# Loads of the step loop on ACT's queue, and the first FFN weights converted and halved earlier

## The chip, the core and the metric

The program runs on one core of one Trainium2 chip. The metric is the device time of one execution in microseconds, taken as the median of several executions. Before the change it is 673.82 us (three runs, 672.1 to 676.8). TensorE (PE) multiplies matrices into the PSUM banks; VectorE (DVE) and ScalarE (ACT) read and write PSUM and SBUF; GpSimd (POOL) works on SBUF here; the DMA engines move data between memory and SBUF. A transfer is issued by an instruction on the queue of one engine: SP's queue, which does nothing else, or those of ACT and POOL, where the instruction stands in line with that engine's computing.

## What is computed

Attention with mixing across heads ("talking heads"), and behind it two feed-forward stages. For 2 batches, 12 heads, 448 positions and head size 64:

```python
scores = scale * np.matmul(q, k.transpose(0, 1, 3, 2))
scores = np.einsum('bhij,hg->bgij', scores, w_pre)        # mix heads before the softmax
attn = np.exp(scores - np.max(scores, axis=-1, keepdims=True))
attn = attn / (np.sum(attn, axis=-1, keepdims=True) + 1e-09)
attn = np.einsum('bhij,hg->bgij', attn, w_post)           # mix heads behind it
x = np.matmul(attn, v)                                    # then laid out as 896 x 768
g = x @ w_gate                                            # 768 x 1536
y = (g * sigmoid(g) * (x @ w_val)) @ w_out                # 1536 x 768
h = y @ w_in                                              # 768 x 2048
out = (h * np.clip(h + 3.0, 0.0, 6.0) / 6.0) @ w_out2     # 2048 x 768
```

The feed-forward (FFN) weights come in as 64-bit numbers and are turned into 32-bit ones on the chip.

## The kernel before

**The loop of steps.** The 2 x 448 query positions are cut into 8 tiles `t` (4 for each batch) and these into 90 chunks of 10 positions; a step takes two chunks, so the loop `for i in range(-LOOK, NP)` has steps 0 to 44 behind a prologue. Three tiles of work are in flight, each at another stage. For its own pair of chunks step `i` does `postmix` (56 matmuls into `ppost`, weights `wn` times exponentials `e`) and copies the result out (`attn_out`, into `at`, half on DVE and half on ACT). For the next pair it has `exps(i+1)` on ACT (tile `e`, with its sums) and `weights(i+1)` on DVE (`rc`, `wn`). For the pair after that it has `premix(i+2)` on PE (`ppre`, from the relaid scores `sx`) and `row_max(i+2)` on DVE (`nm`, which `exps` needs). Beside these a step may hold one head pair of a later tile's scores (`qk`: PE into `pqk`, then one copy each on DVE and ACT into `S`) and one of an earlier tile's product with the values (`av` and `av_rest` on PE into `pav`; `xs` or, in the last two tiles, `xh` on ACT and `xl` on DVE). The second part of `av_rest` waits for a small DVE instruction (`turns`, L348). No step from 36 on has scores. In this document **step i begins with the first matmul of its `postmix`** (L287).

**The order of each engine** is the order in which the code is written (the schedule is manual). What a step does outside its fixed part hangs in the lists `extra[i][place]`; `run(i, place)` writes them out, and `"end"` stands last in a step, behind `out` (`xs`) and before the next step's `exps`.

**Transfers.** `relayout` moves a chunk's scores from `S` into `sx` on SP's queue (104 rows, 182 KB), `relayout_rest` the rest on POOL's (42 KB). Up to six pairs are held in `sx`. The tiles `S0` and `S1` are each used for every second `t`, so the first copy of a new tile's scores waits for all relayouts out of the old one. Loads of queries, keys, values and FFN weights are called from the list `loads` as (step, function, arguments) and go to SP's queue too, between relayouts. In the built program the transfers of SP and ACT share eight semaphore lanes (DMAHW0 to 7) in turn; each waits until the one before it on its lane has landed.

**The first FFN weights.** `fetch`, `convert` and `halve` bring in, convert and split the weights: `convert` is an `Abs` on ACT and four DVE passes (L490), `halve` makes the rounded part on ACT (L427, `hg`, `hv`) and the remainder (`lg`, `lv`; for the first two on POOL). For the first two of the 64 pieces (`j` = 0 and 1: `rg`, `rv`), each cut in thirds, this is spread over steps; one raw tile in the pool `early` serves both. The space of `halve`'s result (`wp0`) is opened at step 41, when the pool of `S` is closed. From then on single FFN matmuls of the first products (`p`, L441) can be put between the attention's: `fill(n)` writes n of them, `FILL` says how many at the last three steps, and two calls `fill(10)` stand in the tail behind the loop. There are 72 in the two products; what is not filled in runs after the tail.

**After the loop** comes a tail with the rest of `av`, and then the FFN: pieces `g`/`v` (12 each), `o` (12), `i` (16) and `p` (18).

Of the kernel before, what the change touches and what calls it, by code (L numbers as in the profile page):

```python
# [9 lines left out]
I64 = mybir.dt.int64  # L10
# [34 lines left out]
FILL = (0, 6, 0)  # L45
# [3 lines left out]
def kernel(  # L49
# [39 lines left out]

    small = kp.tile([128, 8], F32, name="small")  # L90
# [12 lines left out]
    def load_q(t, c0=0, c1=HP, eng=nc.sync):  # L103
        b, i = divmod(t, 4)
        n = ROWS[b][i]
        if c0 == 0:
            qs[t] = pq.tile([128, HP * STRIDE * KI], F32, name=f"q{t}", tag="q")
        base = HP * sum(ROWS[b][:i])
        eng.dma_start(out=qs[t][:, c0 * n : c1 * n], in_=qT[b, :, base + c0 * n : base + c1 * n])

    def load_k(b, c0, c1, eng=nc.sync):
        eng.dma_start(out=ks[b][:, c0:c1, :], in_=kT[b, :, c0 * S : c1 * S].rearrange("p (c j) -> p c j", j=S))
# [4 lines left out]
    def load_v(b, j):  # L117
        nc.sync.dma_start(
            out=vs[b][:, j].rearrange("p h d -> p (h d)"), in_=vv[b, :, j * DM : (j + 1) * DM]
        )  # L120

    new_k(0)
    load_q(0, 0, 2)
    load_k(0, 0, 1, nc.scalar)
    load_k(0, 1, 2)
    load_q(0, 2, 4, nc.scalar)
    load_k(0, 2, 3)
    load_k(0, 3, 4, nc.scalar)
    load_k(0, 4, 5)
    load_q(0, 4, 6, nc.scalar)  # L130
    load_k(0, 5, 6)
    load_q(1)
# [4 lines left out]
    load_q(2)  # L137
    new_v(0)
    for j in range(2):
        load_v(0, j)  # L140
# [258 lines left out]
    def load_w(pool, src, kc, name):  # L399
        st = pool.tile([128, kc, 128], I64, name=f"r{name}", tag="wr", bufs=1 if pool is pools["early"] else 2)  # L400
        n = 2 if pool is pools["early"] else kc
        return st, [(st[:, k : k + n, :], src[:, k : k + n, :]) for k in range(0, kc, n)]
# [70 lines left out]
    def fetch(j, which="wp"):  # L473
        if j < len(subs):
            kind, idx, k0, kc, src = subs[j]
            if j not in raws:
                raws[j] = pools[which], *load_w(pools[which], src, kc, f"{kind}{idx}_{k0}")
            to, of = raws[j][2].pop(0)
            nc.sync.dma_start(out=to, in_=of)

    def convert(j, part=None):
        if j < len(subs):
            kind, idx, k0, kc, _ = subs[j]
            if j not in ys:
                pool, st, _ = raws[j]
                ys[j] = pool, *convert_w(pool, st, kc, f"{kind}{idx}_{k0}")
            todo = ys[j][2]
            for _ in range(len(todo) if part is None else part):
                f, *args = todo.pop(0)
                f(*args)  # L490
# [75 lines left out]
    FREE = {(5, 2): "pqk", (5, 4): "pqk", (6, 0): "pqk", (6, 2): "pqk"}  # L566
# [27 lines left out]
    loads = [(1, load_v, 0, 2), (2, load_v, 0, 3), (3, load_q, 3), (6, load_q, 4)]  # L594
    loads += [(7 + n, load_k, 1, n, n + 1) for n in range(HP)]
    loads += [(15, load_q, 5), (21, load_q, 6), (27, load_q, 7)]
    loads += [(20 + 2 * j, load_v, 1, j) for j in range(JC)]
    loads += [(n, fetch, 0, "early") for n in (14, 17, 19)] + [(n, fetch, 1, "early") for n in (30, 32, 34)]
# [3 lines left out]
    for j in range(2):  # L602
        for n in range(12):
            at_step(17 + 14 * j + n, convert, j, 2 if n % 4 == 0 else 1)
# [10 lines left out]
    for i in range(-LOOK, NP):  # L615
# [25 lines left out]
        if i >= NP - 3:  # L641
            fill(FILL[i - NP + 3])
        run(i, "qk")
        run(i, "out2")
        if i == 41:
            late.close()
            pools["wp0"] = ctx.enter_context(tc.tile_pool(name="wp0", bufs=2, side="right"))
        if i in (42, 43):
            halve(i - 42)
# [9 lines left out]
        while rests < placed and rests // 2 <= i + LOOK + 4 and i > scored[chunks[rests][0]]:  # L659
            relayout_rest(rests)  # L660
            rests += 1
    last = [(6, 4), (6, 5)] + [(7, c) for c in range(HP)]
# [176 lines left out]
```

## Time and profile before

| | before |
|---|---|
| median of three runs | 673.82 us (672.1 to 676.8) |
| the profiled execution: its own time | 673.18 us |
| its span, first to last instruction | 671.4 us |
| PE busy | 660.2 us, 98% |
| DVE, ACT, POOL busy | 499.4, 296.0, 160.3 us |
| granted TensorE clock, mean | 1.000 |

The rest of this text speaks of microseconds from the start of the span. The prologue lasts to 20.56, the loop to 170.49 plus its last step, the tail to 182.80, and the FFN to the end. A matmul's end is modelled, so a "busy" PE may be PE that waits with its last matmul; waits are read from the idle time behind an instruction, `[idle before <-releaser]`, and from the chain of work that ended last.

### The profile page before, as it was taken

How to read it: one execution, taken by the hardware profiler on the slowest of the kernel's cores; microseconds unless marked ns; L12 is line 12 of the kernel's file. 1: busy time of each engine (PE TensorE's matmuls, PEld its weight loads, DVE VectorE, ACT ScalarE, POOL GpSimd, SP SyncE). 2: the span in 40 equal slices, each digit the busy share in tenths (PEclk: the TensorE clock that was granted, in tenths of full speed). 3: DMA queues.
4: the chain of work that ended last, by engine and by line, in shares of the span. 5: the costliest groups of instructions: out<-in, count | busy, mean ns of one | idle time of the engine just before them, and what ended most of it. 6: DMA issues, size and time to landing. Idle time of an engine off the chain costs nothing.

```text
span 671.4 us, 16136 instructions
## 1 busy us (share of the span) xinstructions
PE 660.2 (98%) x6680; PEld 563.2 (84%) x6680; DVE 499.4 (74%) x835; ACT 296.0 (44%) x603; POOL 160.3 (24%) x204
## 2 busy tenths in 40 slices
PE   8989999999999999999999999999999999999997
PEld 3456666666899999999999999999999998999997
DVE  4878889889288888888787666578888888765550
ACT  4667667777234343343432323244444553332220
POOL 3544365445211113111120000013333332000000
PEclk9999999999999999999999999999999999999999
DMA  7767566645023333242333333323222333553420
GB/s 247 213 202 207 189 194 199 184 139 206 12 94 110 127 112 124 95 140 95 108 128 95 108 127 107 128 73 115 95 96 95 108 112 92 167 169 119 152 67 27
DMA packets 35081, 86.87 MB, mean 129 GB/s; under 512 B 10080, under 2 KB 22896, under 8 KB 35008
## 3 DMA queue, kind: packets, MB, share of 16 engines
q1 hardware_dynamic: 26496, 81.21, 37.5%
q0 software_dynamic: 7936, 3.94, 2.4%
q8 instruction: 52, 0.85, 0.5%
q10 hardware_dynamic: 576, 0.70, 0.3%
q14 instruction: 21, 0.17, 0.1%
HBM read 62.37 MB, written 2.75 MB: 97 GB/s over the span
## 4 chain that ended last, share of the span: by engine, by line
PE 76%; DVE 17%; ACT 3%; DMA 3%; issue 1%; SPq 0%; ACTq 0%
PE pp L441 15%; PE po L441 13%; PE pv L441 12%; PE pg L441 12%; DVE yi L490 9%; PE ppost L287 5%; PE ppre L239 5%; PE pqk L171 5%; PE pav L318 5%; DVE rl L727 2%; PE p L441 2%; PE pav L337 2%; DVE yp L490 2%; DVE li L432 2%; ACT hi L427 2%; DMA v<-in_v_dram 1%
## 5 line engine op out<-in xcount | busy, mean ns | idle before, releaser
L441 PE MATMUL pp<-g,hp 128*128 128x448 f32 x384 | 107.8, 362 | 0.0
L703 POOL TENSOR_TENSOR g<-rl,g 128x448 fp32r<-128x448 f32 x32 | 41.3, 1314 | 167.8 <-ACT g L702 167.8
L441 PE MATMUL po<-u,ho 128*128 128x448 f32 x288 | 81.4, 363 | 0.0
L441 PEld LDWEIGHTS pp<-g,hp 128*128 128x128 f32 x384 | 71.9, 187 | 5.4 <-ACT hp L427 0.2
L261 ACT ACTIVATE e<-ppre,nm 128x448 f32<-128x448 f32 x90 | 56.3, 630 | 34.6 <-DVE nm L252 34.5
L441 PE MATMUL pp<-g,lp 128*128 128x448 f32 x192 | 69.7, 363 | 0.2 <-DVE lp L432 0.2
L441 PE MATMUL pi<-x2l,hi 128*128 128x448 f32 x192 | 69.7, 363 | 0.0
L441 PE MATMUL pi<-x2h,hi 128*128 128x448 f32 x192 | 69.6, 362 | 0.0
L441 PE MATMUL pi<-x2h,li 128*128 128x448 f32 x192 | 69.1, 360 | 0.0
L703 POOL TENSOR_TENSOR u<-sg,u 128x448 fp32r<-128x448 f32 x24 | 32.2, 1362 | 148.4 <-ACT u L702 148.4
L220 POOL DMA_DIRECT2D sx<-S x90 | 52.4, 583 | 47.9 <-issue 12.5
L441 PEld LDWEIGHTS po<-u,ho 128*128 128x128 f32 x288 | 54.1, 188 | 3.5
L252 DVE TENSOR_REDUCE nm<-ppre 128x1 f32<-128x448 f32 x90 | 51.8, 617 | 5.0 <-PE ppre L239 3.0
L287 PE MATMUL ppost<-wn,e 60*64 60x60 f32 x2520 | 51.3, 220 | 2.4 <-DVE wn L273 1.7
L441 PE MATMUL po<-u,lo 128*128 128x448 f32 x144 | 51.8, 360 | 0.0
L318 PEld LDWEIGHTS pav<-at,v 128*64 128x64 f32 x576 | 27.9, 136 | 28.4 <-ACT xs L360 15.0
L239 PE MATMUL ppre<-sx,W 64*64 64x448 f32 x360 | 48.8, 544 | 1.4 <-issue 0.7
L287 PEld LDWEIGHTS ppost<-wn,e 60*64 60x64 f32 x2520 | 45.2, 134 | 5.6 <-ACT at L306 3.0
L171 PE MATMUL pqk<-k,q 64*64 64x448 f32 (+3 forms) x384 | 48.5, 552 | 0.3 <-DMA k<-in_k_dram 0.3
L441 PE MATMUL pg<-xl,hg 128*128 128x448 f32 x132 | 47.9, 363 | 0.0
L441 PE MATMUL pv<-xl,hv 128*128 128x448 f32 x132 | 47.9, 363 | 0.0
L441 PE MATMUL pg<-xh,hg 128*128 128x448 f32 x132 | 47.8, 362 | 0.0
(97 smaller groups left out, 1399.6 us busy)
## 6 DMA issues: line engine op xcount, KB each, us to landing
sx<-S SPq DMA_DIRECT2D x90, 182.0 KB
ri<-in_moe_w_in_dram SPq DMA_DIRECT2D x16, 768.0 KB
ro<-in_moe_w_out_dram SPq DMA_DIRECT2D x12, 768.0 KB
rg<-in_moe_w_gate_dram SPq DMA_DIRECT2D x11, 768.0 KB
rv<-in_moe_w_val_dram SPq DMA_DIRECT2D x11, 768.0 KB
rp<-in_moe_w_out_dram SPq DMA_DIRECT2D x12, 640.0 KB
rp<-in_moe_w_out_dram SPq DMA_DIRECT2D x6, 768.0 KB
sx<-S POOLq DMA_DIRECT2D x90, 42.0 KB, 3.9
```

Of the source, the lines that this page charges most:

```text
L171: nc.tensor.matmul(p[e][lo:hi, :S], lhsT=qs[t][r, base + lo : base + hi], rhs=ks[b][r, c, :], start=True, stop=True, tile_position=(64 * e ...
L220: nc.gpsimd.dma_start(out=sx[m // 2][104:128, m % 2, :], in_=rows)
L239: nc.tensor.matmul(p[a][64 * r : 64 * r + 64, :S], lhsT=W1[rows, :], rhs=x[rows, r, :], start=True, stop=True, tile_position=(64 * a, 64 * r),
L252: top = nc.vector.tensor_reduce(nm[:, a : a + 1], pre[i][a][:, :S], AX.X, ALU.max, negate=True)
L261: nc.scalar.activation(e2[a], p[a][:, :S], AF.Exp, bias=nm[:, a : a + 1], scale=1.0, accum_out=sm[:, a : a + 1])
L287: mm = nc.tensor.matmul(p[s][64 * c : 64 * c + 64, at, :, :], lhsT=e2[a][rows, 64 * k : 64 * k + 64], rhs=wn[rows, a, :].rearrange("p (g k ...
L318: nc.tensor.matmul(p[64 * e : 64 * e + 64, : 2 * n], lhsT=vs[b][:, jc, h, :], rhs=ats[t][:, 2 * jc : 2 * jc + 2, h, :n], start=jc == 0, st ...
L337: mm = nc.tensor.matmul(pavs[t, c][64 * e : 64 * e + 64, a * n : a * n + n], lhsT=vs[b][rows, JC - 1, h, :], rhs=ats[t][rows, KB - 1, h, : ...
L427: nc.scalar.copy(hi_flat, y)
L441: nc.tensor.matmul(p[:, :S], lhsT=wt[:, kk, :], rhs=xx, start=start, stop=stop)
L490: f(*args)
L703: eng.tensor_tensor(to[1], src, to[0].bitcast(F32), ALU.subtract)
```

## The change

- The defaults of `load_q`, `load_k` and `load_v` become ACT's queue; the prologue names SP's queue where it used it. So 17 loads of the loop go from SP's queue to ACT's. `fetch` puts the six transfers of the first two weights there as well. Later FFN loads stay on SP.
- The third and fourth part of the first batch's values are loaded at steps 0 and 1 in place of 1 and 2. Three of the six key loads go from steps 10, 11, 12 to 11, 13, 14.
- The first weight is fetched at steps 10, 12, 16 (before 14, 17, 19), the second at 18, 23, 28 (before 30, 32, 34), into a raw tile of its own (pool `second`). They are converted at steps 13 to 24 and 25 to 36 (before 17 to 28 and 31 to 42).
- `second` is closed and `wp0` opened at step 39, and the halves are made at the ends of steps 39 and 42 (before 42 and 43).
- `FILL` has 4 matmuls at step 42 and 6 at step 43 (before 6 at step 43). The `av` of step 43 goes from a `pqk` bank to the one `pav` bank.

```diff
-FILL = (0, 6, 0)
+FILL = {42: 4, 43: 6}
...
-    def load_q(t, c0=0, c1=HP, eng=nc.sync):
+    def load_q(t, c0=0, c1=HP, eng=nc.scalar):
...
-    def load_k(b, c0, c1, eng=nc.sync):
+    def load_k(b, c0, c1, eng=nc.scalar):
...
-    def load_v(b, j):
-        nc.sync.dma_start(
+    def load_v(b, j, eng=nc.scalar):
+        eng.dma_start(
...
-            nc.sync.dma_start(out=to, in_=of)
+            (nc.scalar if j < 2 else nc.sync).dma_start(out=to, in_=of)
...
-    FREE = {(5, 2): "pqk", (5, 4): "pqk", (6, 0): "pqk", (6, 2): "pqk"}
+    FREE = {(5, 2): "pqk", (5, 4): "pqk", (6, 0): "pqk"}
...
-    loads = [(1, load_v, 0, 2), (2, load_v, 0, 3), (3, load_q, 3), (6, load_q, 4)]
-    loads += [(7 + n, load_k, 1, n, n + 1) for n in range(HP)]
+    loads = [(0, load_v, 0, 2), (1, load_v, 0, 3), (3, load_q, 3), (6, load_q, 4)]
+    loads += [(i, load_k, 1, n, n + 1) for n, i in enumerate((7, 8, 9, 11, 13, 14))]
...
-    loads += [(n, fetch, 0, "early") for n in (14, 17, 19)] + [(n, fetch, 1, "early") for n in (30, 32, 34)]
+    loads += [(n, fetch, 0, "early") for n in (10, 12, 16)] + [(n, fetch, 1, "second") for n in (18, 23, 28)]
...
-            at_step(17 + 14 * j + n, convert, j, 2 if n % 4 == 0 else 1)
+            at_step(13 + 12 * j + n, convert, j, 2 if n % 4 == 0 else 1)
...
-        if i >= NP - 3:
-            fill(FILL[i - NP + 3])
+        fill(FILL.get(i, 0))
...
             late.close()
-            pools["wp0"] = ctx.enter_context(tc.tile_pool(name="wp0", bufs=2, side="right"))
-        if i in (42, 43):
-            halve(i - 42)
...
+        if i == 39:
+            second.close()
+            pools["wp0"] = ctx.enter_context(tc.tile_pool(name="wp0", bufs=2, side="right"))
+        if i in (39, 42):
+            halve((i - 39) // 3)
```

SP's queue from step 1 to step 4, before: relayouts `sx` (L204), with the value loads of steps 1 and 2 and the query load of step 3 between them.

```order
L204 DMA sx7_406<-S1_120 104x1x448 [waits DMASW4_49,DMAHW5_49,DMASW3_49,PE_49]
L118 DMA v0_116<-in_v_dram 128x768 [waits DMAHW6_49]
L204 DMA sx7_406<-S1_120 104x1x448 [waits DMAHW7_49,DVE_49]
L204 DMA sx8_470<-S1_120 104x1x448 [waits DMASW7_49,DMAHW0_49,DMASW6_49,PE_49]
L118 DMA v0_116<-in_v_dram 128x768 [waits DMAHW1_49]
L204 DMA sx8_470<-S1_120 104x1x448 [waits DMAHW2_49,DVE_49]
L204 DMA sx9_533<-S1_120 104x1x448 [waits DMASW1_49,DMAHW3_49,DMASW0_49,PE_49]
L109 DMA q3_535<-in_q_dram 128x714 [waits DMAHW4_49]
L204 DMA sx9_533<-S1_120 104x1x448 [waits DMAHW5_49,DVE_49]
```

The same stretch of SP's queue in the changed program: relayouts alone.

```order
L207 DMA sx7_410<-S1_123 104x1x448 [waits DMASW4_49,DMAHW6_49,DMASW3_49,PE_49]
L207 DMA sx7_410<-S1_123 104x1x448 [waits DMAHW7_49,DVE_49]
L207 DMA sx8_474<-S1_123 104x1x448 [waits DMAHW1_49,DMASW7_49,DMAHW4_49,DMASW6_49,PE_49]
L207 DMA sx8_474<-S1_123 104x1x448 [waits DMAHW2_49,DVE_49]
L207 DMA sx9_536<-S1_123 104x1x448 [waits DMASW1_49,DMAHW3_49,DMASW0_49,PE_49]
L207 DMA sx9_536<-S1_123 104x1x448 [waits DMAHW4_49,DVE_49]
```

The three loads have left SP's queue, and no relayout stands behind one.

ACT in steps 2 to 4, before (`e` are the exponentials, `at` and `S` copies out of PSUM):

```order
L306 COPY at0_327<-ppost2_1_417 128x84x5 [waits PE_49]
L187 COPY S0_119<-pqk2_1_1_463 120x448 [waits PE_49]
L261 ACTIVATE e0_124,sm4_476<-ppre4_0_453,nm4_459 128x448 [waits DVE_49,Activation_49]
L261 ACTIVATE e1_125,sm4_476<-ppre4_1_454,nm4_459 128x448 [waits DVE_49,Activation_49]
L306 COPY at0_327<-ppost3_1_480 128x84x5 [waits PE_49]
L187 COPY S0_119<-pqk2_2_1_526 120x448 [waits PE_49]
L261 ACTIVATE e2_126,sm5_541<-ppre5_0_516,nm5_522 128x448 [waits DVE_49,Activation_49]
```

The same place on ACT in the changed program:

```order
L309 COPY at0_330<-ppost2_1_421 128x84x5 [waits PE_49]
L190 COPY S0_122<-pqk2_1_1_467 120x448 [waits PE_49]
L264 ACTIVATE e0_127,sm4_479<-ppre4_0_457,nm4_463 128x448 [waits DVE_49,Activation_49]
L264 ACTIVATE e1_128,sm4_479<-ppre4_1_458,nm4_463 128x448 [waits DVE_49,Activation_49]
L309 COPY at0_330<-ppost3_1_483 128x84x5 [waits PE_49]
L190 COPY S0_122<-pqk2_2_1_529 120x448 [waits PE_49]
L112 DMA q3_538<-in_q_dram 128x714 [waits DMAHW5_49]
L264 ACTIVATE e2_129,sm5_544<-ppre5_0_519,nm5_525 128x448 [waits DVE_49,Activation_49]
```

The query load stands between a step's copies and the next step's exponentials, which wait for it to be issued; the value load of step 1 stands in the same way between that step's `S` copy and `exps(3)`.

DVE in steps 37 and 38, before (`nm` row maxima, `turns` the small instruction that the second part of `av_rest` waits for):

```order
L252 TENSOR_REDUCE nm39_3155<-ppre39_0_3149 128x1 [waits PE_49]
L252 TENSOR_REDUCE nm39_3155<-ppre39_1_3150 128x1 [waits PE_49]
L490 SCALAR_TENSOR_TENSOR yv0_0_2708<-rv0_0_2626,yv0_0_2708 128x256 [waits DMAHW0_49]
L348 MEMSET turns_129 1x1 [waits PE_49]
L306 COPY at6_2928<-ppost38_0_3180 128x84x5 [waits PE_49]
L269 TENSOR_SCALAR rc39_3214<-sm39_3167 128x2 [waits Activation_49]
```

And in the changed program:

```order
L255 TENSOR_REDUCE nm39_3165<-ppre39_0_3159 128x1 [waits PE_49]
L255 TENSOR_REDUCE nm39_3165<-ppre39_1_3160 128x1 [waits PE_49]
L351 MEMSET turns_132 1x1 [waits PE_49]
L309 COPY at6_2940<-ppost38_0_3189 128x84x5 [waits PE_49]
L272 TENSOR_SCALAR rc39_3223<-sm39_3176 128x2 [waits Activation_49]
```

The conversion pass between the row maxima and `turns` is gone from this step, as it is from all of steps 37 to 42.

## Rows read from the trace of the kernel before

**Rows 1.** Page, part 1: engine, busy us (share), instructions.
```profile
PE 660.2 (98%) x6680; PEld 563.2 (84%) x6680; DVE 499.4 (74%) x835; ACT 296.0 (44%) x603; POOL 160.3 (24%) x204
```
**Rows 2.** Stages: length, busy PE, PEld, DVE, ACT, POOL, clock, DMA share, GB/s.
```profile
20.56:38.61 18.05, 15.23 (x375) 8.65 (x375) 14.69 (x37) 12.40 (x34) 8.54 (x16) 1.00 0.77 213
146.02:170.49 24.47, 23.74 (x674) 16.40 (x673) 21.11 (x65) 17.30 (x51) 14.15 (x21) 1.00 0.47 162
182.80:437.00 254.20, 254.20 (x1271) 238.29 (x1272) 195.63 (x241) 90.89 (x134) 32.19 (x24) 1.00 0.34 112
```
**Rows 3.** Chain that ended last, step 19: start us, us, what.
```profile
87.23 0.76 PE ppost L287 x52
88.09 0.81 PE ppre L239 x8
90.68 0.76 PE ppost L287 x52
```
**Rows 4.** Chain of waits at step 4, and PE's timeline there.
```profile
29.07 9.48 DMA v<-in_v_dram
...
38.59 0.26 PE L337 MATMUL pav<-at,v 64*64 64x50 f32 x2 [1.99 <-DMA v<-in_v_dram]
```
**Rows 5.** Timeline of ACT and PEld, steps 1 to 4: start, us, engine, line.
```profile
23.67 0.63 ACT L261 ACTIVATE e<-ppre,nm 128x448 f32<-128x448 f32 x1 [0.95 <-DVE nm L252]
26.26 0.53 ACT L187 COPY S<-pqk 120x448 f32<-120x448 f32 x1 [0.76 <-PE pqk L171]
26.69 0.64 ACT L261 ACTIVATE e<-ppre,nm 128x448 f32<-128x448 f32 x1
34.97 0.19 PEld L171 LDWEIGHTS pqk<-k,q 64*64 64x64 f32 x6 [0.52 <-ACT S L187]
```
**Rows 6.** Timeline of the queues: one load's issue on ACT, one on SP.
```profile
1.18 0.45 ACTq L109 DMA_DIRECT2D q<-in_q_dram  x1
96.38 1.35 SPq L109 DMA_DIRECT2D q<-in_q_dram  x1
```
**Rows 7.** Value loads' issues (ns min/median/max); relayouts on POOL's queue to landing.
```profile
L118 SPq DMA_DIRECT2D v<-in_v_dram x8: 328/548/1113, 7.6 to 113.8; - x8
DMA to landing us min/median/max: 2.8/3.9/7.5
```
**Rows 8.** Groups on ACT, 20 to 170 us: busy, mean ns, idle before.
```profile
L261 ACT ACTIVATE e<-ppre,nm 128x448 f32<-128x448 f32 x88 | 55.0, 630 | 31.9 <-DVE nm L252 31.9
```
**Rows 9.** Chain of waits and ACT's timeline at the end of step 31.
```profile
127.19 4.64 DMA rv<-in_moe_w_val_dram
...
131.86 0.44 ACT L490 ACTIVATE yv<-rv 128x256 f32<-128x256 f32 x1 [1.41 <-DMA rv<-in_moe_w_val_dram]
```
**Rows 10.** PE's timeline: beginnings of steps 32, 33, 36, 37 and 44.
```profile
131.99 0.28 PE L287 MATMUL ppost<-wn,e 60*64 60x60 f32 x2
135.79 0.28 PE L287 MATMUL ppost<-wn,e 60*64 60x60 f32 x2
...
146.02 0.28 PE L287 MATMUL ppost<-wn,e 60*64 60x60 f32 x2
148.66 0.28 PE L287 MATMUL ppost<-wn,e 60*64 60x60 f32 x2
...
170.49 0.28 PE L287 MATMUL ppost<-wn,e 60*64 60x60 f32 x2
```
**Rows 11.** Timeline of DVE and PE, step 43.
```profile
167.26 0.77 DVE L490 SCALAR_TENSOR_TENSOR yv<-rv,yv 128x256 uint32<-128x256 uint32 x1
168.10 0.32 PE L337 MATMUL pav<-at,v 64*64 64x55 f32 x4 [0.17 <-DVE turns L348]
```
**Rows 12.** Chain that ended last: filled FFN matmuls, first product.
```profile
168.43 1.41 PE p L441 x6
...
182.80 9.41 PE p L441 x46
```
**Rows 13.** Chain that ended last: a stretch without a visible wait.
```profile
69.85 0.60 issue
```

More of the change, by code (lines that the diff above doesn't have):

```diff
@@ L88 @@
     ctx.enter_context(tc.tile_pool(name="shift", bufs=1, side="right")).tile([128, 80], F32, name="shift1")
+    second = ExitStack()
+    pools["second"] = second.enter_context(tc.tile_pool(name="second", bufs=1, side="right"))
     small = kp.tile([128, 8], F32, name="small")
@@ L122 @@
     new_k(0)
[L123 to L132, printed above, removed]
+    load_q(0, 0, 2, nc.sync)
+    load_k(0, 0, 1)
+    load_k(0, 1, 2, nc.sync)
+    load_q(0, 2, 4)
+    load_k(0, 2, 3, nc.sync)
+    load_k(0, 3, 4)
+    load_k(0, 4, 5, nc.sync)
+    load_q(0, 4, 6)
+    load_k(0, 5, 6, nc.sync)
+    load_q(1, eng=nc.sync)
     W1 = cst.tile([128, 64], F32, name="W1")
@@ L136 @@
     nc.sync.dma_start(out=W2.rearrange("p g k -> p (g k)"), in_=w_post)
-    load_q(2)
+    load_q(2, eng=nc.sync)
     new_v(0)
     for j in range(2):
-        load_v(0, j)
+        load_v(0, j, nc.sync)
     Ss = [psc.tile([128, H + 1, S], F32, name=f"S{i}") for i in range(2)]
@@ L399, in load_w @@
     def load_w(pool, src, kc, name):
-        st = pool.tile([128, kc, 128], I64, name=f"r{name}", tag="wr", bufs=1 if pool is pools["early"] else 2)
-        n = 2 if pool is pools["early"] else kc
+        ahead = pool is not pools.get("wp")
+        st = pool.tile([128, kc, 128], I64, name=f"r{name}", tag="wr", bufs=1 if ahead else 2)
+        n = 2 if ahead else kc
         return st, [(st[:, k : k + n, :], src[:, k : k + n, :]) for k in range(0, kc, n)]
@@ L485, in convert @@
                 pool, st, _ = raws[j]
+                pool = pools["early"] if j < 2 else pool
                 ys[j] = pool, *convert_w(pool, st, kc, f"{kind}{idx}_{k0}")
```

## The prediction

> **What bounds the kernel now.** The page's busy time comes first: PE is busy for 98% of the span [rows 1], so only time in which PE waits can be won. The stages say where that can be. In the FFN PE is full from 182.80 on [rows 2], and nothing of the change touches work behind that but four matmuls. In the loop PE is short of the stretch in two places: 15.23 of 18.05 us in steps 0 to 4, and 23.74 of 24.47 in steps 36 to 43 [rows 2]; since a matmul's end is modelled, the second shortfall is larger than it looks, and the beginnings of steps show it better. In the middle the chain runs through PE alone: from one `postmix` to the next 3.45 us in step 19, which holds a conversion pass on DVE, scores and `av` [rows 3]. What DVE, ACT and the queues do there is hidden, as long as it fits into 3.45.
>
> Three waits interrupt this. At step 4 the chain of waits leaves PE for a value load: issued at 29.07, landed 9.48 us later, with PE idle for 1.99 before the first `av_rest` [rows 4]. At step 31 ACT stands for 1.41 before `Abs` until the first third of `rv`, fetched a step earlier, has landed after 4.64 [rows 9]; the next step takes 135.79 - 131.99 = 3.80 [rows 10]. And steps 36 to 43 take 170.49 - 146.02 = 24.47, while step 36 itself, PE alone, takes 148.66 - 146.02 = 2.64 [rows 10].
>
> **Values sooner, on ACT's queue: steps 0 to 4.** The load that PE waits for is issued at the end of step 1 behind ACT's `S` copy, near 26.7 instead of 29.07. Even if it took 9.48 again it would land at 36.2, before PE's wait began (38.59 - 1.99 = 36.60). The wait goes: **-1.99**.
>
> What it costs is ACT's time. One issue took 0.45 on ACT's own queue in the prologue; on SP's queue the shortest took 0.33, the median value load 0.55, and the longest load in the loop 1.35 [rows 6, 7]. I take 0.55, since the loop is busier than the prologue, with 0.33 and 1.35 as bounds. The load of step 0 falls into the 0.95 in which ACT waits for `nm` before `exps(2)` and costs nothing [rows 5]. The one of step 1 has no cover: `exps(3)` starts at 26.69, as soon as the `S` copy of 26.26 lets go [rows 5], and `weights(3)`, then `postmix(3)`, wait for it. The query load of step 3 stands in the same way before `exps(5)`; behind that come ACT's `at` and `S` copies, and PE's weight load already waits 0.52 for such a copy at 34.97 [rows 5]. Two issues on the path: **+1.1** (0.66 to 2.7).
>
> The load of step 0 also moves 384 KB, at the stretch's 213 GB/s [rows 2] 1.8 us of all DMA engines, beside the last relayouts out of `S0`, which the `S` copies of step 1 wait for. Before, it was issued at step 1 behind them on one queue. Nothing in the trace shows how the two queues share: bounds 0 and 1.8. ACT's copy at 26.26 waited for PE [rows 5], so there is some margin left; I take **+0.4**. On this the rows are unsure: a relayout on POOL's queue took from 2.8 to 7.5 us to land, 3.9 at the median [rows 7], with SP's queue full beside it. The Trainium skill (DMA: Bandwidth & Descriptors, Queues, rings and completion order) says that each DMA engine takes turns between the queues that have work, packet by packet. By that rule the relayouts would be slowed for the whole 1.8 and the sum below would be 671.2; by the quickest landing of these rows the term would be 0 and the sum 669.4. The steps so far come to -1.99 + 1.1 + 0.4 = **-0.5**.
>
> **The other loads on ACT's queue.** Fifteen loads and six fetches follow, at steps 6 to 28, between `xs` and the next `exps`. There ACT waits for `nm`: 31.9 us over 88 exponentials, two in a step [rows 8], so 31.9 / 44 = 0.73 a step. An issue of 0.55 lies inside. At steps 13 and 21 an `Abs` of 0.44 [rows 9] stands in the same gap, 0.26 too much; but the exponentials of a step are used by the next step's `postmix`, and PE does not notice. Behind a waiting load on ACT's queue stand `exps`, then DVE's `rc`, `wn` and `nm`. Each load waits for the transfer eight before it on the shared lanes; at some 2.5 transfers a step that is three steps old, 10 us against the 9.48 of the worst landing. **0**. If an issue took 1.35 everywhere, 21 x (1.35 - 0.73) = 13 would be the other bound. SP's queue gets emptier; its relayouts run steps ahead, and I count nothing for it.
>
> **Early weights.** With `rv` fetched from step 18 and converted from step 25, ACT does not stand at step 31, and step 32 takes 3.45 like its neighbours: **-0.35**. Steps 13 to 16, 29 and 30 get passes that they did not have; step 19 shows such a step at PE's pace [rows 3], so 0.
>
> **Steps 36 to 43.** No scores are left here; PE needs 2.64 a step, but DVE's conversion passes (0.77 for one [rows 11]) delay `turns`, the copies and `nm`. At step 43 PE waits for `turns` [rows 11]. PE's own need: seven steps of 2.64 = 18.48; step 43 without a `premix` (0.81 [rows 3]) but with six filled matmuls (1.41 [rows 12]) 3.24; together 21.72, so 24.47 - 21.72 = 2.75 is waiting. The passes end at step 36 in the changed kernel, and the halves sit in ACT's gaps (0.9 and less for one `hg`). The four matmuls at step 42 take 4 x 0.2 plus about 0.2 for the switch (1.41 - 6 x 0.2); 0.8 comes back from the product at 182.80, which has 42 left of 46 at 9.41 / 46 = 0.2 [rows 12]. They also cover the wait of `av` at step 43 for the single `pav` bank. -2.75 + 0.2 = **-2.5**. If the chain from `nm` over `exps`, `at`, `xh`, `xl` to the next `nm` still sets steps 41 to 43, half of it stays: -1.2 at worst.
>
> **Sum.** -0.5 - 0.35 - 2.5 = -3.35. Against the profiled execution's own 673.18 that is 669.8; that execution lies 0.64 below the median of the runs, 673.82, so a new median may be 670.5. I predict 670.1.
>
> **Rivals.**
> - *The start gives nothing back.* The wait for the values is replaced at step 1: the `S` copies wait for the relayouts out of `S0` (+1.8), and the two issues cost 0.55 each. -1.99 + 1.1 + 1.8 = +0.9, with the rest 673.18 + 0.9 - 0.35 - 2.5 = 671.2. For it speaks that the DMA engines carry 213 GB/s there [rows 2]; against it that ACT's copy waited for PE, not for a transfer. The sharing by turns that the Trainium skill states (same page and section) is this case.
> - *ACT becomes the bound: slower.* In steps 6 to 28 the issue on ACT exceeds ACT's gap of 0.73. From a mean issue of 0.73 + 3.35 / 21 = 0.89 on, the gain is gone; at 1.1 it is 21 x 0.37 = 7.8 lost, 673.18 - 3.35 + 7.8 = 677.6. For it: 1.35 was seen on SP [rows 6]; against it the median of 0.55, and that ACT's exponentials are early.
> - *More than counted.* The chain also has stretches in which PE waits for nothing that the profile shows, 0.60 at 69.85 for one [rows 13]. If the new order of transfers also clears a few of these (about 1.8 us for three) and the start costs only 0.66 for its issues: -1.99 + 0.66 - 0.35 - 2.75 - 1.8 = -6.2, 667.0.
>
> **How the numbers follow.** Chances: the forecast (668.5 to 671) 0.55; the start gives nothing back 0.23; ACT the bound 0.08; more than counted 0.14. The range goes from 667.5, which leaves out more than half of the last case, to 674.0, where the start costs its worst bounds (-1.99 + 2.7 + 1.8 = +2.5) and steps 36 to 43 give only 1.2: 673.18 + 2.5 - 0.35 - 1.2 = 674.1. The likeliest case alone has 668.5 to 671. One per cent of the time, 6.7 us, is about what a measurement of this kernel can tell from no change. Faster by that needs the whole last case and more: 0.09. Slower by that needs an issue above 1.2 us on ACT: 0.03. Within: 0.88.
>
> **What would show it.** Right: no idle before the first `av_rest`; step 32 at about 3.4; steps 36 to 41 at 2.64; ACT's `exps(3)` and `exps(5)` each about half a microsecond later against their step; 42 matmuls in the first product. Wrong: `S` copies at step 1 released by a relayout; ACT's exponentials released by its own queue in steps 7 to 28, with steps above 3.45; steps 38 to 41 still near 2.9, released by DVE or ACT. The prediction fails if an issue on ACT is far from 0.55, or if transfers on two queues hinder each other more than 1.8 us' worth.

## The result and the profile after

The changed kernel took **677.03 us** (median of 20 executions, 672.72 to 682.79) against 672.78 for the kernel before beside it (20 executions): ratio **1.0063, 95% interval 1.0044 to 1.0082**, so about 4.25 us slower, where 670.1, some 3.7 us faster, was forecast. Slower is sure, but by less than the one per cent that the chances speak of. The profiled execution took 676.66 us. (The ratios on record are not always the quotient of the medians beside them.)

The page of the changed kernel: busy time, the granted TensorE clock in slices, the queue that carries PE's program (so read under e6), and the shares of the chain that ended last.

```profile
span 674.9 us, 16125 instructions
PE 661.2 (98%) x6680; PEld 564.1 (84%) x6680; DVE 500.7 (74%) x835; ACT 296.9 (44%) x603; POOL 160.0 (24%) x204
PEclk9999999998999999999999999999999999999999
q8 instruction: 52, 0.85, 0.5%
PE 75%; DVE 17%; ACT 2%; DMA 2%; issue 2%; POOL 1%; SPq 0%; POOLq 0%; ACTq 0%
```

Busy time tells nothing against [rows 1]. But the slice from 152 to 169 us has an 8 in the row of the clock. The windows by stage (columns: us, busy time of each engine with its count, granted clock, share of the DMA engines, GB/s), to be held against [rows 2]:

```profile
19.24:37.73 18.49, 15.76 (x375) 8.64 (x375) 14.81 (x37) 11.32 (x31) 8.73 (x16) 1.00 0.77 224
145.83:174.79 28.96, 25.87 (x678) 17.45 (x677) 20.63 (x60) 17.15 (x50) 16.46 (x24) 0.94 0.39 137
```

Steps 0 to 4 take 18.49 instead of 18.05, and steps 36 to 43 take **28.96 instead of 24.47**, at a mean clock of 0.94. Steps 5 to 35 take 108.10 where they took 107.41 (from the beginnings of `postmix` in the two timelines). From step 0 to step 44 that is 155.55 against 149.93, 5.62 more; 0.8 is given back by the four matmuls that the first product no longer has, and the profiled execution reached step 0 1.32 sooner. What is left, 3.5, is the difference of the spans, 674.9 - 671.4.

So the loss lies in steps 36 to 43, where the gain was forecast. Their lengths, from the beginnings of `postmix`:

| step | 36 | 37 | 38 | 39 | 40 | 41 | 42 | 43 | sum |
|---|---|---|---|---|---|---|---|---|---|
| before | 2.64 | 2.92 | 2.82 | 3.34 | 2.79 | 2.91 | 3.36 | 3.69 | 24.47 |
| after | 2.64 | 3.05 | 2.64 | 4.17 | 4.41 | 4.06 | 4.00 | 4.00 | 28.96 |

Here is where step 40 of the changed kernel stands still: rows of the timelines of DVE, POOL, PE and ACT, in the brackets the engine's idle time and what ended it. First the same place in the kernel before, then the changed kernel:

```profile
159.67 0.16 DVE L269 TENSOR_SCALAR rc<-sm 128x2 f32<-128x2 f32 x1
160.06 0.28 DVE L273 TENSOR_TENSOR wn<-W,rc 128x120 f32<-128x120 f32 x1
160.53 0.35 PE L287 MATMUL ppost<-wn,e 60*64 60x60 f32 x2
```

```profile
159.59 0.60 DVE L309 COPY at<-ppost 128x420 f32<-128x420 f32 x1 [0.81 <-PE pav L340]
160.09 1.95 POOL L434 TENSOR_TENSOR lg<-yg,hg 128x384 fp32r<-128x384 f32 x2
160.10 1.98 DVE L272 TENSOR_SCALAR rc<-sm 128x2 f32<-128x2 f32 x1
162.12 0.17 DVE L273 RECIPROCAL rc<-rc 128x2 f32<-128x2 f32 x1
162.32 0.28 DVE L276 TENSOR_TENSOR wn<-W,rc 128x120 f32<-128x120 f32 x1
162.75 1.20 PE L290 MATMUL ppost<-wn,e 60*64 60x60 f32 x53 [1.51 <-DVE wn L276]
163.23 0.63 ACT L264 ACTIVATE e<-ppre,nm 128x448 f32<-128x448 f32 x1 [2.80 <-DVE nm L255]
```

POOL's part of the half that step 39 ends with is `lg` (the remainder of the first FFN weight, 1.95 us in two passes). It begins at 160.09, in step 40. DVE's `rc` for step 41, two columns wide, begins at 160.10 and takes **1.98 us**; in undisturbed steps of the two kernels it takes 0.16 to 0.17. `wn` is late, and PE stands for 1.51 before `postmix` of step 41. `lg` was meant to wait its turn (`pool_turn`: behind `wn`, while DVE reads PSUM), but the `wn` that it waits for, the one for step 40, was done a step ago (157.42); POOL reached `lg` late, behind a split of `x` and a relayout, just as the next `rc` was due.

What follows is on PE. Windows of the changed kernel, columns as above:

```profile
160.00:162.00 2.00, 1.24 (x20) 0.77 (x16) 2.00 (x2) 0.43 (x2) 1.98 (x3) 1.00 0.27 84
162.00:163.00 1.00, 0.26 (x5) 0.17 (x5) 0.93 (x4) 0.00 (x0) 0.04 (x1) 1.00 0.00 0
163.00:164.00 1.00, 1.00 (x61) 0.98 (x63) 0.67 (x3) 0.77 (x3) 0.00 (x0) 1.00 0.27 49
164.00:165.00 1.00, 1.00 (x13) 0.20 (x4) 0.85 (x3) 1.00 (x4) 0.00 (x0) 0.63 0.71 246
165.00:166.00 1.00, 1.00 (x10) 0.51 (x8) 1.00 (x4) 0.17 (x2) 0.57 (x2) 0.50 1.03 422
166.00:167.00 1.00, 1.00 (x18) 0.73 (x17) 0.54 (x2) 0.90 (x3) 0.86 (x1) 0.50 1.01 399
167.00:168.00 1.00, 1.00 (x55) 1.00 (x55) 0.06 (x1) 0.44 (x2) 0.00 (x0) 0.67 0.95 393
```

After the wait the granted clock goes from 1.00 (2.4 GHz) to 0.50 (1.2 GHz) for some 3.4 us, from 164.3 to 167.7, and back. `pav` of step 41 and `postmix` of step 42 take 1.37 and 1.30 there (0.79 and 1.03 to 1.11 before). Step 41 is 1.15 longer than before. The second half, `lv`, ends at 171.8 and is followed on POOL by a split of `x`; the last `rc` (172.53) takes 0.78, and PE waits 0.69 for DVE's `xl` at 174.06. Finally, in step 39 PE stands for 0.78 with nothing to wait for that the profile shows ("issue").

So of the 4.49: step 40 1.62, step 41 1.15, step 39 0.83, step 43 0.31, step 42 0.64 with the four filled matmuls (0.8) in it, and steps 36 to 38 together -0.05.

At the beginning, rows that answer [rows 4, 5]: ACT's and PE's timeline in steps 1 and 4.

```profile
25.19 0.53 ACT L190 COPY S<-pqk 120x448 f32<-120x448 f32 x1 [1.01 <-DMA sx<-S]
25.21 0.33 ACTq L121 DMA_DIRECT2D v<-in_v_dram  x1
...
35.40 0.59 PE L242 MATMUL ppre<-sx,W 64*64 64x448 f32 x2 [1.84 <-issue]
```

The wait of `av_rest` for the values [rows 4] is gone. In its place PE stands for 1.84 in `premix` of the same step with an empty "issue". The issue on ACT takes 0.33 and lies beside ACT's own copy. And `postmix` of steps 32 and 33, against [rows 10]: 135.65 - 132.26 = 3.39 instead of 3.80.

```profile
132.26 0.28 PE L290 MATMUL ppost<-wn,e 60*64 60x60 f32 x2
135.65 0.28 PE L290 MATMUL ppost<-wn,e 60*64 60x60 f32 x2
```

### The profile page after: what moved, and what is told of

The parts are those of the page before. It is cut to its first block, busy times and chain, and to the rows that moved or that the text cites. A ratio compares the mean times of both kernels' runs of the same rounds, so it can differ in the third digit from the quotient of the medians.

```text
span 674.9 us, 16125 instructions
## 1 busy us (share of the span) xinstructions
PE 661.2 (98%) x6680; PEld 564.1 (84%) x6680; DVE 500.7 (74%) x835; ACT 296.9 (44%) x603; POOL 160.0 (24%) x204
## 4 chain that ended last, share of the span: by engine, by line
PE 75%; DVE 17%; ACT 2%; DMA 2%; issue 2%; POOL 1%; SPq 0%; POOLq 0%; ACTq 0%
PE pp L445 15%; PE po L445 13%; PE pg L445 12%; PE pv L445 12%; DVE yi L495 9%; PE ppost L290 5%; PE ppre L242 5%; PE pav L321 5%; PE pqk L174 4%; DVE rl L733 2%; PE pav L340 2%; PE p L445 2%; DVE yp L495 2%; DVE li L436 2%; ACT hi L431 2%
## 5 line engine op out<-in xcount | busy, mean ns | idle before, releaser
L242 PE MATMUL ppre<-sx,W 64*64 64x448 f32 x360 | 51.0, 549 | 2.3 <-issue 1.8
```

What stands on the lines that cost most here:

```text
L242: nc.tensor.matmul(p[a][64 * r : 64 * r + 64, :S], lhsT=W1[rows, :], rhs=x[rows, r, :], start=True, stop=True, tile_position=(64 * a, 64 * r),
```

## The experiments

Two theories stood first. **A**: `lg` of the half at the end of step 39 holds DVE's small passes in step 40, PE stands, its clock falls; that is the loss. **B**: the loads on ACT's queue disturb the relayouts and with them steps 0 to 36. A third, **C**, came out of the first four traces and is told with e6. All were timed beside runs of the kernel before.

**e1: the halves back to steps 42 and 43,** and with them the fill of step 42 and the bank of step 43's `av`.

```diff
-FILL = {42: 4, 43: 6}
+FILL = {43: 6}
...
-    FREE = {(5, 2): "pqk", (5, 4): "pqk", (6, 0): "pqk"}
+    FREE = {(5, 2): "pqk", (5, 4): "pqk", (6, 0): "pqk", (6, 2): "pqk"}
...
         if i == 41:
             late.close()
+            second.close()
+            pools["wp0"] = ...
+        if i in (42, 43):
+            halve(i - 42)
...
-        if i in (39, 42):
-            halve((i - 39) // 3)
```

> The changed kernel with the two halves at steps 42 and 43 and the fills (6 at step 43) as before; loads on ACT's queue, early values and early conversions stay. Theory A (POOL's remainder lg of step 39 holds DVE's rc for 1.98 us instead of 0.17, PE then stands 1.51 us and its granted clock falls to 0.5 for some us): the loss of 4.25 us goes, 672 to 673; rc at 0.2 us everywhere, steps 39 to 43 at 2.7 to 3.4 each. Rival B (the loads on ACT's queue disturb relayouts and premixes in steps 0 to 36): still 676 to 677.

Measured: 673.29 us (12 executions), before 672.50; ratio 1.0016 (0.9990 to 1.0042). `rc` takes 0.16 in every step from 39 on. Most of the loss is gone with the halves alone, as A says and B doesn't. But in the profiled execution (677.22, one of the three slowest of the 12) steps 39 and 42 took 6.41 and 5.95, and steps 36 to 43 together 30.38, more than in the changed kernel; so A's picture of quiet steps failed. PE stood in the middle of a `postmix` with nothing to issue, for 1.87 and 2.44. PE's row, and the windows around it:

```profile
167.73 0.39 PE L290 MATMUL ppost<-wn,e 60*64 60x60 f32 x10 [2.44 <-issue]
```
```profile
165.00:166.00 1.00, 0.29 (x15) 0.15 (x5) 0.22 (x2) 1.00 (x4) 0.63 (x1) 1.00 1.03 416
166.00:167.00 1.00, 0.00 (x0) 0.00 (x0) 0.00 (x0) 0.13 (x2) 0.00 (x0) 1.00 0.40 154
167.00:168.00 1.00, 0.27 (x15) 0.27 (x19) 0.00 (x0) 0.00 (x0) 0.00 (x0) 1.00 0.05 18
```

All DMA engines were busy with FFN loads when it began.

**e2: only the queue undone.**

```diff
-    def load_q(t, c0=0, c1=HP, eng=nc.scalar):
+    def load_q(t, c0=0, c1=HP, eng=nc.sync):
...
```

`load_k`, `load_v` and `fetch` likewise.

> The changed kernel with the queue alone undone: all loads of the loop go through SP's queue again, at the steps of the change; halves at 39 and 42 stay. Theory A (the remainder on POOL against DVE's rc at step 39): still 676 to 678, steps 39 to 43 still near 4 us each. Rival B (the loads on ACT's queue): 672 to 673, and the S copies of step 1 are no longer released by a relayout. Third case, that SP's queue with more loads at steps 0 and 1 holds the relayouts back: above 678.

Measured: 675.91 us, before 672.50; ratio 1.0043 (1.0017 to 1.0069). The loss stays without ACT's queue. The `wn` for step 41 took 2.42 beside `lg`, and steps 40 to 43 took 5.02, 4.19, 5.13 and 3.92. For A, against B.

**e3: the queue alone, put into the kernel before.**

```diff
-    def load_q(t, c0=0, c1=HP, eng=nc.sync):
+    def load_q(t, c0=0, c1=HP, eng=nc.scalar):
...
```

`load_k`, `load_v` and the early fetches likewise.

> The kernel before with the queue alone changed: its loads of the loop go through ACT's queue, at its own steps; halves, fills and conversions as before. Theory A: 671.5 to 673, so no loss; with the 0.33 us that an issue took on ACT in the trace of the change, ACT stays ahead. Rival B: 675 to 677, with S copies of steps 1 to 4 released by relayouts.

Measured: 673.27 us, before 672.50; ratio 1.0002 (0.9978 to 1.0026). Loads on ACT's queue show no effect that can be told from none (-1.5 to +1.7 us). As the cause of 4.25 us, B is out.

**e4: the first half one step later.**

```diff
-        if i in (39, 42):
-            halve((i - 39) // 3)
+        if i in (40, 42):
+            halve((i - 40) // 2)
```

> The changed kernel with the first halve at step 40 instead of 39, so that the two parts of lg wait for wn(41), run beside nm on PSUM, and meet no rc. Theory A: rc at 0.2 to 0.4 us in steps 39 to 42, PE does not stand for 1.5 us, clock stays near 1.0; 672.5 to 674. If not the meeting of lg and rc but the earlier halves as such (hg on ACT, the fetches that they release) cost the time: 676 to 677, the granted clock of steps 40 to 43 still near 0.5 to 0.7.

Measured: 674.37 us, before 672.50; ratio 1.0013 (0.9990 to 1.0035). `lg` now lies behind `wn`, and no `rc` before step 43 is above 0.25. One step of one number gives most of the loss back. The other half of A's expectation failed here too: PE did stand for 2.29 in `postmix` of step 41, behind its first four matmuls, and the clock did fall, though `wn` had been there for 2.8 us when PE went on. Steps 36 to 43 took 28.55. Nothing is named for this wait:

```profile
158.68 0.25 DVE L272 TENSOR_SCALAR rc<-sm 128x2 f32<-128x2 f32 x1
159.16 0.28 DVE L276 TENSOR_TENSOR wn<-W,rc 128x120 f32<-128x120 f32 x1
159.96 1.94 POOL L434 TENSOR_TENSOR lg<-yg,hg 128x384 fp32r<-128x384 f32 x2 [0.50 <-ACT hg L431]
162.23 1.66 PE L290 MATMUL ppost<-wn,e 60*64 60x60 f32 x52 [2.29 <-issue]
```

**e5: POOL's pass alone, put into the kernel before.** Two subtractions of the shape of `lg`'s parts, started when DVE's `at` copy of step 40 ends.

```diff
...
+        if i == 40:
+            spare = psx.tile([128, 2, S], F32, name="spare", tag="sx")
...
+            for r in range(2):
+                of = nc.gpsimd.tensor_tensor(spare[:, r, :384], y0[...], y0[...], ALU.subtract)
+                tc.add_manual_dep(of.ins, copied[40], in_turn, reason="meets rc")
```

> The kernel before with two subtractions on POOL added at step 40, of the shape of lg's parts (128x384 each, y minus y into a spare tile; their result is used by nobody), started when DVE's at copy of step 40 ends, so that they run beside rc, its reciprocal and wn. Nothing else differs. Theory A (POOL's pass holds DVE's small passes between SBUF tiles, PE stands, its clock falls): one of rc, reciprocal or wn takes about 1.9 us, postmix of step 41 is late by 1.5 to 2 us, and the time is 2 to 4.5 us above before: 674.5 to 677. If the hold is a chance of one execution, or PE catches up: 672 to 673.5, the small passes at 0.2 to 0.4 us.

Measured: 675.03 us, before 673.40; ratio 1.0022 (0.9996 to 1.0049), so some 1.5 us, of which the interval leaves -0.3 to 3.3. The place itself is plain (timeline of POOL, DVE and PE):

```profile
157.75 1.62 POOL L669 TENSOR_TENSOR spare<-yg 128x384 f32<-128x384 f32 x2
157.65 1.86 DVE L273 TENSOR_TENSOR wn<-W,rc 128x120 f32<-128x120 f32 x1
159.66 0.55 PE L287 MATMUL ppost<-wn,e 60*64 60x60 f32 x8 [1.23 <-DVE wn L273]
```

`wn` is held as long as POOL works, and step 40 takes 4.33 instead of 2.79. In this execution the clock didn't fall in the loop, neither after this wait of 1.23 nor after one of 1.69 for nothing in step 42. Over all its executions the clock fell about as often as beside it in the kernel before (in 5 of 12 and in 9 of 28, counted as further below). So about 1.5 us stand for the hold by itself, as far as the interval allows, and the rest of the 4.25 needs the fall of the clock and the second hold.

**e6: FFN loads held back (theory C).** The gaps named "issue" in all traces so far lie at one kind of place. Counting PE's instructions (weight loads, matmuls and the some 90 of its sequencer) in order of their start, those over 0.3 end at 3.75, 10.76, 12.75, 16.76, 17.75, 21.75, 28.75, 29.75 or 30.76 times 256, and nowhere else. The page counts 52 packets, 0.85 MB, on the queue of the kind "instruction", 16 KB each; PE's 13,360 weight loads and matmuls over 52 are 257. **C**: PE's program comes by blocks of 256 instructions through the same DMA engines as the data, and a block that stands behind data leaves PE with nothing to issue.

```diff
...
-    fetch(2)
+    fetch(2, then=begun_at)
```

`then` makes the DMA wait for the last `postmix`, and the next load stands behind it on SP's queue; the first half stands at step 40, as in e4.

> The changed kernel with the first halve at step 40, and with the first two loads of FFN weights that follow the early ones (768 KB each, issued near step 41) held until the last postmix of the loop. Theory C (PE's program arrives by blocks of 256 instructions through the DMA engines; a block that queues behind loads leaves PE at a fixed place of the program with nothing to issue): no issue gap at the block limits of steps 41 and 42 (they were 2.29 us in e4 and 2.44 in e1), the granted clock stays at 1.0 there, 671.5 to 673.5. If the loads have no part in it: as e4, 673.5 to 675, with gaps of 1 to 2.5 us at one of the limits in steps 39 to 42.

Measured: 674.91 us, before 673.40; ratio 1.0012 (0.9988 to 1.0035), as e4. At the limits of steps 41 and 42 PE had no such wait, and the clock stayed at 1.00 through steps 36 to 43, which took 26.31 instead of 28.55. But a wait of 1.32 stood at the limit before (step 39), where no FFN load ran, and others in steps 4 and 28. The waits at step 42's limit fit the loads: over 0.3 in six of the eleven traces with the loads running there, in none of the three with the loads held (e6, c1, c2), which are few. The total didn't move, so C's time was missed.

**e7: PE's program shifted by 64 instructions.**

```diff
+        for _ in range(32):
+            nc.tensor.matmul(p[:, :16], lhsT=ones[0], rhs=ones[1][:, :16], start=True, stop=True)
```

> The changed kernel with 32 tiny matmuls (128x16) more at the very start, so 64 instructions of PE (a weight load and a matmul each) ahead of everything. Work that the reference doesn't need, but harmless; the prologue may take 1 to 3 us more. Theory C (blocks of 256 instructions): the places at which PE has nothing to issue, 0.75 of a block after a multiple of 256 in all six traces so far, lie 64 instructions earlier in the program of the loop (in the middle of another group of matmuls), and none is left at the old places. If they are waits of the kernel's own that the trace fails to name, they stay at the same premix and postmix as before.

Measured, one execution: 681.43 us. This tells A and C apart in one trace. The waits for nothing stayed at 0.76 of a block and so moved 64 instructions up in the program. At step 22 the second execution of the kernel before (b2, below) waits in `premix` at 98.69; with the shift the wait is in `postmix` of the same step. At step 24 six of the traces wait in `postmix`; with the shift it is `premix` of step 23. The wait for the `wn` of step 41 stayed at the beginning of that `postmix`, now 64 instructions off any block limit. First b2, then e7:

```profile
98.69 1.09 PE L239 MATMUL ppre<-sx,W 64*64 64x448 f32 x8 [0.78 <-issue]
105.79 0.98 PE L287 MATMUL ppost<-wn,e 60*64 60x60 f32 x52 [0.92 <-issue]
```
```profile
99.98 0.62 PE L290 MATMUL ppost<-wn,e 60*64 60x60 f32 x26 [1.26 <-issue]
106.16 0.72 PE L242 MATMUL ppre<-sx,W 64*64 64x448 f32 x3 [1.34 <-issue]
...
166.55 1.62 PE L290 MATMUL ppost<-wn,e 60*64 60x60 f32 x56 [1.89 <-DVE wn L276]
```

Where a block was waited for, PE went on 1.2 to 1.7 us after the block's packet had ended: so in all 39 waits over 0.3 us that the 14 traces name "issue" on PE from step 2 to step 43. In the holds that lie at a limit (the change, e2, e5, e8, a2) the block had come 2.5 to 4.9 us before; those are A's.

**e8: the values at steps 1 and 2 again.**

```diff
-    loads = [(0, load_v, 0, 2), (1, load_v, 0, 3), ...
+    loads = [(1, load_v, 0, 2), (2, load_v, 0, 3), ...
```

> The changed kernel with the two value loads of the loop at steps 1 and 2 again instead of 0 and 1, still through ACT's queue; all else as in the change, the halves at 39 and 42 too. The prediction's step (values sooner gives back 1.99 us at step 4): 678 to 679, with the wait of the first av_rest for v back. What the traces of the change suggest (the start is held up by transfers in either case, 18.05 us for steps 0 to 4 before and 18.49 after): within 1 us of the changed kernel, 676 to 678, steps 0 to 4 at 18 to 19 us.

Measured: 676.86 us, before 673.40; ratio 1.0032 (1.0010 to 1.0054). Taking the sooner values back doesn't make it slower; steps 0 to 4 took 17.95. The step of the prediction that gave 1.99 back for sooner values is refuted. The hold is there (`wn` 2.41), but this trace parts it from the fall of the clock: behind PE's wait of 2.15 for `wn` the clock stayed at 1.00, and step 41 took 2.89, as before (2.91). It fell at 169.09, at the end of a wait of 2.43 for a block in step 42. PE's rows and the windows behind the two waits:

```profile
162.86 1.24 PE L290 MATMUL ppost<-wn,e 60*64 60x60 f32 x53 [2.15 <-DVE wn L276]
169.19 0.58 PE L290 MATMUL ppost<-wn,e 60*64 60x60 f32 x10 [2.43 <-issue]
```
```profile
162.86:165.75 2.89, 2.86 (x82) 1.88 (x82) 2.36 (x9) 1.95 (x6) 0.25 (x1) 1.00 0.74 255
169.19:172.50 3.31, 3.31 (x27) 1.82 (x28) 2.40 (x7) 1.77 (x4) 1.13 (x2) 0.50 0.02 5
```

**b2 and a2: both kernels once more, unchanged,** for a second profiled execution each.

> The kernel before, unchanged, for a second profiled execution, since the first one had only two waits for program blocks (0.60 and 0.72 us). If those waits come by chance of the transfers (theory C): others than in the first, at the same 0.75 of a block, 1 to 5 us in sum between steps 2 and 43; steps 36 to 43 between 24.5 and 28 us. No small pass of DVE above 0.5 us in either case (theory A).

> The changed kernel, unchanged, for a second profiled execution. Theory A: one of rc, reciprocal and wn of step 41 takes about 2 us again and postmix of step 41 waits 1.3 us or more, since the order of POOL's queue makes it so and not chance; the rc of step 43 about 0.7 us again. Theory C: the waits for program blocks lie elsewhere than in the first. If the long rc was chance: 0.2 to 0.4 us here.

Measured: 674.33 and 675.76 us, one execution each. In b2 steps 36 to 43 took 24.61 (24.47 the first time) with no small pass above 0.37; the block waits lay at steps 14 and 22, as in the first, and at 11 and 24 besides. In a2 the hold is there again, and the block had been there for 4.9 us. DVE, POOL and PE of a2:

```profile
158.19 2.42 DVE L276 TENSOR_TENSOR wn<-W,rc 128x120 f32<-128x120 f32 x1
158.51 1.95 POOL L434 TENSOR_TENSOR lg<-yg,hg 128x384 fp32r<-128x384 f32 x2
160.75 0.96 PE L290 MATMUL ppost<-wn,e 60*64 60x60 f32 x23 [2.37 <-DVE wn L276]
```

Together: in all five traces with the first half at step 39 (both of the change, e2, e7, e8) one of the small passes takes 1.98 to 2.42, and steps 36 to 43 take 28.96 to 30.70. In four of them the clock goes to 0.50 with PE's wait for `wn`, and step 41 takes 4.06 to 4.36; in e8 it doesn't, and step 41 takes 2.89. In none of the other traces but e5, where it was made so, does a small pass take over 0.87. The length of steps 36 to 43 in one execution doesn't tell the kernels apart, though: block waits alone made 30.38 of it in e1 and 28.55 in e4.

The many executions do. The mean granted clock is on record for each; one stretch of 3.4 us at 0.50 brings it to 0.997. It is 0.997 or less in 17 of the 20 executions of the changed kernel, in 9 of 12 of e2 and 11 of 12 of e8; with the first half later, in 6 of 12 (e1) and 7 of 12 (e4, e6 each); in the kernel before, in 20 of the 89 timed beside the experiments. Of the 35 beside e1 to e4, the 5 with a fall took 3.0 us more than the other 30 (means 675.49 and 672.46), the waits ahead of the fall included. The three executions of the changed kernel without a fall took 674.20 in the mean, 1.7 more than those 30. An estimate from these: some 1.7 of the 4.25 without a fall, which agrees with e5, and (17/20 - 20/89) x 3.0 = 1.9 by falls that come more often. In e3 the clock fell in 6 of 12, without a loss that could be told from none; the cause is open.

**c1: all that the runs speak for.** e6, with values at steps 1 and 2, the last splits of `x` behind `wn(43)`, and the second conversion one step sooner.

```diff
...
-        if i + 1 in weighed:
+        if min(i + 1, NP - 1) in weighed:
...
-            at_step(13 + 12 * j + n, convert, ...
+            at_step(13 + 11 * j + n, convert, ...
```

> The changed kernel with what the runs so far speak for, at once: first half at step 40, the two large FFN loads held until the last postmix of the loop, values at steps 1 and 2, the last two splits of x on POOL at step 43 made to wait for wn(43) (so that they no longer run beside the last rc, 0.6 to 0.8 us in several traces), and the conversion of the second early weight one step sooner (its last pass delayed turns at step 37, 3.05 instead of 2.64 us). Theory A with C: none of DVE's small passes above 0.4 us, step 37 at 2.64, waits for PE's program blocks as by chance; 671 to 673.5, so level with before or up to 0.2% better. If something of the change that no run has undone alone (the earlier fetches and conversions of the weights) costs time: 674 to 676.

Measured: 672.71 us, before 673.59; ratio 0.9993 (0.9969 to 1.0017). Level with before, so the change's loss is mended, and its gain isn't there. Steps 36 to 43:

```profile
146.00:170.42 24.42, 24.05 (x679) 16.75 (x677) 18.31 (x59) 16.90 (x50) 15.90 (x24) 1.00 0.29 98
```

24.42 with the four filled matmuls in it, so 23.6 against the 24.47 of before.

**c2: fewer loads beside the relayouts of steps 22 and 23.**

```diff
-    ... (n, fetch, 1, "second") for n in (18, 23, 28)]
+    ... (n, fetch, 1, "second") for n in (18, 26, 29)]
-    loads += [(20 + 2 * j, load_v, 1, j) for j in range(JC)]
+    loads += [(i, load_v, 1, j) for j, i in enumerate((20, 24, 26, 27))]
```

> c1 with two loads taken out of steps 22 and 23, where the transfers take 0.8 to 1.0 of the DMA engines: the second value load of the second half at step 24 instead of 22, the following two at 26 and 27, and the two last thirds of rv at steps 26 and 29 instead of 23 and 28. Theory C: the wait for the program block at step 24 (1.64 us in c1, 1.75 in the second execution of the change, 0.92 in the second of before) is gone or under 0.5 us, and the time is 1 to 2 us below c1, 670.5 to 672.5. If the block waits for the relayouts and not for the loads: a wait of 0.9 to 1.8 us at the same place, the time as c1, 672 to 674.

Measured: 679.64 us (6 executions), before 673.27; ratio 1.0094 (1.0078 to 1.0111). Both expectations missed the time. The block wait at step 24 stayed, 1.41, as the second of them says, though the transfers around the block took 0.58 to 0.61 of the DMA engines from 96 to 100 instead of 0.82 to 0.85 in c1. So what the block stands behind there isn't the loads that were moved; whether it is the relayouts wasn't tried. And the last value load now came too late, which made a wait of its own:

```profile
102.84 0.98 PE L290 MATMUL ppost<-wn,e 60*64 60x60 f32 x52 [1.41 <-issue]
...
123.70 0.27 PE L340 MATMUL pav<-at,v 64*64 64x60 f32 x2 [3.04 <-DMA v<-in_v_dram]
```

Issued at 116.56 and needed at 123.70 - 3.04 = 120.66, it landed 7.09 after its issue. The clock fell behind this wait (124.14), and steps 28 and 29 took 7.53 and 5.04 instead of c1's 3.40 and 3.39. So c2's time says nothing on theory C.

## Why the prediction was wrong, step by step

**Steps 36 to 43, -2.5: the step that failed.** The prediction put the halves into ACT's gaps and counted `hg` alone. A half is also two passes on POOL of 1.95 together, and they had no term. Those of step 39's half ran in step 40 and met DVE's `rc` or `wn` for step 41. What stood in the place of -2.5 was +4.49 in the profiled execution, or +3.7 with the 0.8 that came back later: the hold, the clock at 1.2 GHz behind it, the second hold, and a block wait. In front of the prediction lay a line of the code that points to it, the reason of `pool_turn`, "POOL reads SBUF while DVE reads PSUM". The Trainium skill says it outright (SBUF — State Buffer, section "Who interferes with whom"): VectorE and GpSimd share a port pair, an exclusive lock that whoever issues first has for the whole instruction, while the other blocks fully; the page says so for DVE's 2-port modes and for a DVE instruction with two inputs from SBUF, as `wn` is. The traces agree on the full block: `rc` 1.98 and `wn` 2.42 beside POOL's 1.95, which is two instructions, and DVE didn't get in between them. Who issued first they don't show: by its recorded start `wn` was 0.32 ahead of `lg` in a2. Even without holds the term was too large: c1 gives 0.85, the prediction's bound was 1.2. The steps were counted at PE's own 2.64, but 37, 39 and 40 of c1 took 2.85, 2.78 and 3.19. Nor are steps 37 to 42 free of conversion passes, as the prediction counts: the last one, written at the end of step 36, runs in step 37 (149.23, 0.42), which takes 3.05 instead of 2.92.

**The value wait, -1.99: right at its place, wrong for the time.** `av_rest` doesn't wait any more, and steps 0 to 4 didn't become shorter. The 1.99 was also the largest of three: the same wait took 0.51 in b2 and 0.77 in e5, whose loads are those of the kernel before. In three traces with sooner values (the first of the change, e1, e6) PE waits instead for its third program block in `premix` of step 4 (1.84, 1.30, 1.47), and in e3, with loads on ACT's queue at the old steps, 2.12. In e1, e4, e7 and a2 an `S` copy waits 1.6 to 2.6 for relayouts, and step 2 takes 4.28, 4.73, 4.82 and 3.92 instead of 3.02; but step 2 takes 4.06 in b2 too, the kernel before, without such a wait, so not all of this is the change's. Over steps 0 to 7 the kernel before took 27.93 and 27.49 (e5 26.76), the changed one 28.64 and 27.10, e8 27.83. This is the time of the rival "the start gives nothing back", by two ways of which it named one.

**Issues on ACT, +1.1: mis-sized.** 0.33 each, beside ACT's running copy; in e3 the whole queue shows no cost. The rival "ACT becomes the bound" had no part: idle before the exponentials is 32.8 us from 20 to 170 us, against 31.9 [rows 8].

**Relayouts beside the value load, +0.4: right in the first trace, too small in others.** ACT's `S` copy of step 1 waited 1.01 for one, which is the prediction's own sign of being wrong, and step 2 took 3.30 instead of 3.02. In the four traces named above step 2 shows 0.9 to 1.8. The turn-taking of the queues that was cited there could not be told from other causes by these runs.

**The wait for `rv`, -0.35: right.** Step 32 takes 3.39 in place of 3.80, and so in every trace with the earlier fetches.

**The other loads, 0: right** in e3, as far as its interval goes. (The list has fourteen of them, not fifteen; the bound of 13 becomes 12.4, and nothing else changes.) **"More than counted"**, fewer empty "issue" waits: they are waits for program blocks, which fall partly at other limits in every execution, and no run got the total below the kernel before by moving loads (e6, c2). The first trace of before had two of them and was taken for the rule.

What remains open: how the 4.25 divide exactly between the hold (e5: about 1.5, with an interval that reaches zero; 1.7 from three executions) and the falls of the clock, why one wait is followed by a fall and another isn't, and which transfers a late block stands behind.

## What to carry to other kernels

Cost a moved step on every engine that it uses, and look at what the *other* engine does at that moment: a POOL pass between SBUF tiles can hold a two-column DVE pass for its whole length (here 1.98 us in place of 0.16). A dependency that puts work in its turn must name the turn in which the work will really run, and not one that is long past when its queue comes to it. A gap named "issue" at fixed places of a long program is worth counting in blocks of instructions before one looks for its cause in the data, and one profiled execution is too few to say which of these gaps a kernel has.

## What the runs showed of the hardware

- POOL's `lg` (two passes of 128x384, 1.95 us) held a DVE pass of 128x2 for 1.98 and one of 128x120 for 2.42; the reductions `nm` from PSUM (1.15 for two) kept their time beside it (c1, at 159.95).
- In steps 0 to 43 of the 14 traces TensorE's granted clock went to 0.50 (1.2 GHz) eleven times, for 3.4 us each, in or up to 1.5 us behind waits of 1.51 to 3.04 us. After other waits of that length it stayed at 1.00: 1.99 (before, step 4), 2.12 (e3, step 4), 2.15 (e8, step 41), 2.66 (e4, step 29). So the length of one wait doesn't tell whether it falls.
- PE's program came in 52 packets of 16 KB. PE went on 1.2 to 1.7 us after a late block had ended, and waited up to 2.66 us for one (e4, step 29). The Trainium skill (Runtime: NRT & Kernel Launch, section "Instruction fetch mechanics") gives the 16 KiB blocks and calls the cost of crossing a limit mostly hidden; the traces agree on the blocks and, by number, on "mostly": 39 of some 400 crossings between steps 2 and 43 of the 14 traces cost a wait of over 0.3 us.
- An issue on ACT's queue took 0.33 us (23 in the trace of the change), beside ACT's running copy.
